# Fused chunked attention and low-rank mixer: blocked q, k, e and u in HBM, transposed on VectorE

## The chip, the cores and the metric

One core of one Trainium2 chip runs the whole program, in one launch. The metric is the device time in microseconds. A core has five engines with queues of their own, each worked through in order: TensorE (PE, with its weight loads shown as PEld), VectorE (DVE), ScalarE (ACT), GpSimd (POOL) and SyncE (SP). SyncE issues nearly all DMAs. All data are float32; `fp32r` is float32 read by TensorE in its faster form, so values are split into a rounded part and a rest ("high" and "low").

## The reference

Eight batches, eight heads, 576 positions of 64 channels. Attention runs within chunks of 64 positions; its output, laid side by side by head, is the input x (576 x 512 per batch) of a mixer:

```python
scores = scale * np.matmul(q_c, k_c.transpose(0, 1, 2, 4, 3))   # per chunk of 64
scores = scores - np.max(scores, axis=-1, keepdims=True)
attn = np.exp(scores)
attn = attn / (np.sum(attn, axis=-1, keepdims=True) + 1e-09)
out = np.matmul(attn, v_c)
...
xt = x.transpose(0, 2, 1)
h = xt @ U @ V                      # along the 576 positions, rank 32
u = x + h.transpose(0, 2, 1)
ch = np.maximum(u @ w_ch1, 0.0) @ w_ch2     # 512 -> 2048 -> 512
return (u + ch).astype(np.float32)
```

U, V, w_ch1 and w_ch2 arrive as 64-bit floats; the kernel makes float32 of their words itself.

## The kernel before

**Tiles.** Batches go in four pairs. A pair has 2 x 576 = 1152 rows, nine tiles (t = 0 to 8) of 128 rows. Three tiles make a group g. The hidden layer is cut into 16 blocks f of 128. The unit of the large work is a block (pair, group, f): `hidden` (L682) does 12 matmuls `h` (three products of high and low parts for four channel blocks), `relu_high` (L696, ScalarE) and `relu_low` (L701, VectorE) make `hh` and `hl`, and `project_out` (L708) adds nine matmuls `o` of the block before. There are 4 x 3 x 16 = 192 blocks.

**Side work per tile.** Attention of a tile (`attention_ops`, L441): load q, k and v; turn q and k so that channels lie on partitions; scores `sc` (16 small matmuls, PE); maximum and subtraction (DVE, two of each); `exp` (ACT); turn e = exp(...) so that keys lie on partitions; `av` (PE); the sums and the scaling into x (DVE). Then `project_ops` (L580) forms y = U-product over five tiles of a batch, from x split into `xh` and `xl`, and `mix_ops` (L634) forms u = x + V-product (`low_rank`, `add`), turns u so that channels lie on partitions (`transposed`), and splits it into `uth` and `utl`, the operands of `h`. So u of a group must be ready, turned and split, before that group's first block.

**How things are turned.** The nine tiles of pair 0 are `early`: q, k, e and u are turned on TensorE with the identity (four 128 x 128 blocks each) into a PSUM bank, and copied out by ScalarE. For the 27 later tiles q and k are first copied inside HBM (`halve`, L379) into arrays by half head (32 channels), from which 8 DMAs per tile and operand put 32 x 32 squares where VectorE's 32 x 32 transposition (`squares`, L458) makes the turned form of them. Such a copy reads and writes pieces of 128 bytes. The e and u of later tiles are turned on TensorE like the early ones (L452 with output `ps_eT`, L656 with output `ut`).

**Order.** The first part (pair 0's attention and mixing, the conversion of 16 weight blocks W0 to W15, and the blocks of groups 0 and 1 of pair 0 between them, `STRETCHES`) is laid out by a small planner (`order`, L146) from written costs and places, and kept as planned. Each weight block is loaded raw by SyncE (`wraw`, two DMAs of 512 KB), then converted by seven VectorE and two ScalarE passes. Pair 1's halving copies are put on SyncE's queue after each block from the fourth on (`HALVES_FROM`), and wait there for the block (`add_manual_dep`). Tiles 0 and 1 of pair 1 are attended at blocks 28 and 30 (`GATES`). From pair 0's group 2 on, a loop (L909) emits one block after the other and in four slots per block a share of a list of side steps made by `attend`, `mixes` and `proj`; the framework's scheduler then decides the final order on each engine from these priorities and its own estimate of when inputs are there.

**Buffers.** Eight slots of one pool (`NS`) hold all turned and raw operands of the side work, ten hold x (`NX`), eight PSUM banks hold all results of TensorE.

Of the kernel before, what the change touches and what calls it, by code (L numbers as in the profile page):

```python
# [21 lines left out]
def kernel(  # L22
# [99 lines left out]
    ROOM = {"bank": 8, "w": NF, "slot": NS, "x": NX, "y": 2, "ut": 2, "h": 2, "mx": 2, "sm": 2}  # L122
# [198 lines left out]
    def w_ops(f, after=None):  # L321
# [15 lines left out]
        for z in range(n):  # L337
            cols = slice(z * size, (z + 1) * size)

            def room(z=z):  # L340
                return wslot((size,), U32, f"wroom_{f}") if n == 1 else slot(U32, f"wroom_{f}_{z}")
# [13 lines left out]
            tag = "w" if n == 1 else "slot"  # L355
# [14 lines left out]

    loaded = {}
# [6 lines left out]
    hidden_last = [None]  # L378

    def halve(b, z, g):  # L380
        d = halves[b, z, g] = dram.tile([S, H * SQ], F32, name=f"half{'qk'[z]}_{b}_{g}")
        moved = nc.sync.dma_start(
            d.rearrange("s (h i) -> s h i", h=H),
            (q, k)[z][b, :, :, g * SQ : (g + 1) * SQ].rearrange("h s i -> s h i"),
        )
        sync = mybir.DependencyInfo(mybir.DependencyClass.Sync, mybir.DependencyReason.DATA)
        tc.add_manual_dep(moved.ins, hidden_last[0].ins.name, sync, reason="after this block")

    def halvings(pr):
        return [lambda b=b, z=z, g=g: halve(b, z, g) for b in (2 * pr, 2 * pr + 1) for z in range(2) for g in range(2)]  # L390

    def load_qk(pr, t):
        n = f"{pr}_{t}"
        if early(pr, t):
            words = wslot((4 * DM,), F32, "qkv_" + n)
            qn, kn = (words[:, z * DM : (z + 1) * DM].rearrange("p (h d) -> p h d", h=H) for z in range(2))
            vn = words[:, 2 * DM : 2 * DM + H * D1].rearrange("p (c a k) -> p c a k", c=2, k=D1)
        else:
            qn = slot(F32, "qn_" + n, (P, P // SQ, P))
            kn = slot(F32, "kn_" + n, (P, P // SQ, P))  # L400
            vn = slot(F32, "vn_" + n, (P, 2, HP, D1))
        nc.gpsimd.memset(vn[:, :, :, D:], 1.0)  # L402
        if not early(pr, t):
            for z, dst in enumerate((qn, kn)):
                for r, m, b, s0 in segments(pr, t):
                    for e in range(2):
                        for g in range(2):
                            x0 = (2 * e + g) * SQ
                            nc.sync.dma_start(
                                dst[x0 : x0 + SQ, r // SQ : (r + m) // SQ, :],  # L410
                                halves[b, z, g][s0 : s0 + m, e * P : (e + 1) * P].rearrange(
                                    "(a j) c -> j a c", j=SQ
                                ),
                            )
            loaded[pr, t] = qn, kn, vn
            return
# [5 lines left out]
    def heads(pr, t, e):  # L422
        return slice(e, None, 2) if early(pr, t) else slice(e * HP, (e + 1) * HP)
# [19 lines left out]

    def attention_ops(pr, t, *after):
        n = f"{pr}_{t}"
        st = {}
        mine = early(pr, t)

# [9 lines left out]
        def squares(z, name):  # L458
            dst = slot(F32, name + n, (P, HP, P))
            nc.vector.transpose(  # L460
                dst.rearrange("p h (a j) -> p h a j", j=SQ),
                loaded[pr, t][z].rearrange("p a (h i) -> p h a i", i=SQ),
# [3 lines left out]
        def evacuate(name):  # L466
            if name[0] == "e":
                dst = slot(F32, name + n, (P, HP, P))
# [22 lines left out]
        def maximum(e):  # L491
            if e == 0:
                st["ex"] = slot(F32, "ex_" + n, (P, HP, 2, C))
# [4 lines left out]
        def subtract(e):  # L498
            mx = st["mx"][:, e, :]
            nc.vector.tensor_sub(st["ex"][:, :, e, :], st["sc"][e], mx.unsqueeze(2).broadcast_to([P, HP, C]))  # L500

        def exp():
            exf = st["ex"].rearrange("p a b k -> p (a b k)")
            nc.scalar.activation(exf, exf, AF.Exp, scale=SCALE)  # L504

# [22 lines left out]
        def scaled(e):  # L528
# [12 lines left out]
        flat = lambda: st["ex"].rearrange("p a b k -> p (a b k)")  # L541
        lq = Op(
            "SP", 3.4 if mine else 5.0, lambda: load_qk(pr, t), *after, take="w" if mine else "slot slot slot", lat=1.6
        )
        if mine:
            tq = Op("PE", 0.55, lambda: transpose(src(0), "qT_"), lq, begun.get((pr, t - 2)), take="bank")
        else:
            tq = Op("DVE", 0.6, lambda: squares(0, "qT_"), lq, begun.get((pr, t - 2)), take="slot")
# [9 lines left out]
        if mine:  # L558
            cq = Op("ACT", 0.58, lambda: evacuate("qT_"), tq, take="w", free="bank")
            tk = Op("PE", 0.55, lambda: transpose(src(1), "kT_"), lq, tq, take="bank")  # L560
            ck = Op("ACT", 0.58, lambda: evacuate("kT_"), tk, cq, free="bank")
            turned = [[tq, cq], [tk, ck]]
        else:
            ck = Op("DVE", 0.6, lambda: squares(1, "kT_"), tq, take="slot")
            turned = [[tq], [ck]]
        sc = Op("PE", 0.62, scores, ck, take="bank bank", free="w" if mine else "slot slot slot slot")
        m0 = Op("DVE", 0.41, lambda: maximum(0), sc, take="slot mx")
# [4 lines left out]
        te = Op("PE", 0.55, lambda: transpose(flat(), "eT_"), ex, take="bank", free="slot")  # L572
        ce = Op("ACT", 0.58, lambda: evacuate("eT_"), te, take="slot", free="bank")
        av = Op("PE", 0.65, values, ce, lv, take="bank bank x", free="slot w" if mine else "slot slot")
# [4 lines left out]
        return [[lq, lv], *turned, [sc, m0, s0, m1, s1, ex], [te, ce], [av, sm, x0, x1]]  # L579
# [4 lines left out]
    def project_ops(pr, e, xs):  # L584
        steps = []
        prev = None
        for i in range(5):
# [3 lines left out]
            def high(i=i, n=n, st=st):  # L591
                st["h"] = slot(F32R, "xh_" + n)
                nc.scalar.copy(st["h"], x_of[pr, i + 4 * e])  # L593

            def low(i=i, n=n, st=st):
                st["l"] = slot(F32R, "xl_" + n)
# [22 lines left out]
            h = Op("ACT", 0.62, high, xs[i + 4 * e], take="slot")  # L619
            lo = Op("DVE", 0.69, low, h, take="slot")  # L620
            prev = Op("PE", 0.47, product, lo, prev, u_done, take="" if i else "bank", free="slot slot")
# [12 lines left out]
    def mix_ops(pr, t, x, ys, after=None, first=None):  # L634
# [22 lines left out]

        def high():
# [23 lines left out]
    def hidden(pr, g, f):  # L682
# [5 lines left out]
        for cc in range(NCC):  # L688
            for z, u in prods:
                hidden_last[0] = nc.tensor.matmul(  # L690
                    ps[:, :GN], lhsT=w[:, z, cc], rhs=u[:, cc, :], start=(n == 0), stop=(n == 3 * NCC - 1)
                )
                n += 1
        return ps
# [78 lines left out]
    HALVES_FROM = 4  # L773
# [36 lines left out]
    second = halvings(1)  # L810
    gates = dict(zip(GATES, range(len(GATES))))
    for g, f0, f1 in STRETCHES:
        for f in range(f0, f1):
# [5 lines left out]
            if blocks >= HALVES_FROM and second:  # L819
                rank[0] = 0  # L820
                in_halves = Op("SP", 0.6, second.pop(0), prev[0], lat=6.0)
            if blocks in gates:
                assert not second
                rank[0] = 0
                attention_ops(1, gates[blocks], prev[0], in_halves)
# [11 lines left out]
    Op("SP", 3.8, lambda: load(1, len(GATES)), prev[0], take="slot slot slot")  # L837
# [13 lines left out]
    to_halve = {}  # L851
# [10 lines left out]
    def step(*group):  # L862
        return lambda: [o.run() for o in group]

    def attend(ts):
        steps = []
        prev = None
        for key in ts:
            i = tiles.index(key)
            _, q, k, sc, et, av = attention_ops(*key)  # L870

            def ahead(i=i):
# [84 lines left out]
```

## Time and profile before

| what | value |
|---|---|
| runs of the kernel | 986.68 us median of 3 (986.33 to 990.02) |
| the profiled execution: its time | 984.5 us |
| its span, first to last instruction | 982.7 us |
| mean granted TensorE clock | 0.990 |
| busy: PE, DVE, ACT | 98%, 45%, 23% of the span |
| first matmul of a hidden block | 64.5 us |
| DMA packets, bytes | 208123, 70.58 MB |

A profile gives each instruction's line in the kernel, its engine, what it writes and reads, and its time. "Idle before, releaser" is how long its engine had stood before it and what ended that. The chain of waits goes back from the last instruction to whatever released each step, so its shares tell what the time was spent on. The clock column is the share of full speed that TensorE was granted. Ends of matmuls are modelled, since they overlap: the chain gives better prices for them than their mean duration does.

### The profile page before, as it was taken

The page shows a single profiled execution, that of the slowest core. Times are in us where ns is not written, and L with a number is a line of the kernel's source. Part 1 is how long each engine was busy: PE and PEld are TensorE (multiplying, and loading weights), DVE is VectorE, ACT ScalarE, POOL GpSimd, SP SyncE. Part 2 cuts the span into 40 slices and gives each one's busy share as a digit, 9 for nine tenths or more (in the row PEclk, how much of TensorE's full clock was granted, in tenths as well). Part 3 has the DMA queues.
Part 4 walks back from the last instruction along what each step waited for, and adds up shares of the span by engine and source line. Part 5 has one row for each costly group of instructions (what it writes and reads, how often), then busy time and mean ns, then how long its engine had stood idle before and what let it go on. Part 6 is the DMA issues. An engine that isn't in the chain of part 4 may idle for free.

```text
span 982.7 us, 16528 instructions
## 1 busy us (share of the span) xinstructions
PE 961.3 (98%) x6854; PEld 835.0 (85%) x6857; DVE 439.5 (45%) x867; ACT 227.5 (23%) x406; POOL 33.7 (3%) x89
## 2 busy tenths in 40 slices
PE   7899899999999999999999999999999999999998
PEld 4569799988888889888888888888888889999997
DVE  5789789874442534233443343333433333211211
ACT  4543333321321211111211221111212121111110
POOL 6500000000000000000000000000000000000000
PEclk8999999999999999999999999999999999999999
DMA  9945964146753121433332111111121000000000
GB/s 218 224 140 97 210 187 139 36 133 112 129 107 89 31 41 52 81 61 86 68 79 62 28 33 37 42 37 48 42 57 33 33 1 1 33 1 1 33 1 33
DMA packets 208123, 70.58 MB, mean 72 GB/s; under 512 B 164768, under 2 KB 200640, under 8 KB 208048
## 3 DMA queue, kind: packets, MB, share of 16 engines
q1 hardware_dynamic: 206528, 66.35, 29.9%
q0 software_dynamic: 1520, 3.17, 1.6%
q8 instruction: 54, 0.88, 0.4%
q14 instruction: 21, 0.17, 0.1%
HBM read 59.98 MB, written 23.67 MB: 85 GB/s over the span
## 4 chain that ended last, share of the span: by engine, by line
PE 91%; DMA 3%; DVE 3%; ACT 1%; SPq 1%; issue 1%; POOL 0%; DVEq 0%; ACTq 0%; POOLq 0%
PE h L690 41%; PE o L716 40%; PE sc L482 2%; PE av L513 2%; PE ut L656 2%; PE ps_eT L452 1%; DMA wraw<-in_moe_w_ch_dram 1%; PE u L644 1%; DMA qkv<-in_k_dram 1%; PE y L604 1%; PE y L605 1%; DMA uraw<-in_moe_U_dram 1%; DMA qkv<-in_v_dram 1%; PE y L611 1%; ACT qkT L474 0%
## 5 line engine op out<-in xcount | busy, mean ns | idle before, releaser
L690 PE MATMUL h<-uth,w 128*128 128x384 f32 x1536 | 424.8, 341 | 0.0
L716 PE MATMUL o<-w,hh 128*128 128x512 f32 x1152 | 359.2, 401 | 3.7 <-ACT hh L698 3.5
L690 PEld LDWEIGHTS h<-uth,w 128*128 128x128 f32 x1536 | 282.1, 188 | 8.2 <-issue 0.2
L703 DVE SCALAR_TENSOR_TENSOR hl<-h,hh 128x384 fp32r<-128x384 f32 x192 | 106.5, 555 | 361.3 <-ACT hh L698 361.1
L690 PE MATMUL h<-utl,w 128*128 128x384 f32 x768 | 260.0, 339 | 0.0
L716 PEld LDWEIGHTS o<-w,hh 128*128 128x128 f32 x1152 | 211.6, 189 | 42.2 <-ACT hh L698 5.6
L716 PE MATMUL o<-w,hl 128*128 128x512 f32 x576 | 217.7, 397 | 0.0
L698 ACT ACTIVATE hh<-h 128x384 fp32r<-128x384 f32 x192 | 94.2, 491 | 499.9 <-PE h L690 499.6
L690 PEld LDWEIGHTS h<-utl,w 128*128 128x128 f32 x768 | 144.8, 189 | 6.1 <-DVE utl L669 0.3
L716 PEld LDWEIGHTS o<-w,hl 128*128 128x128 f32 x576 | 108.7, 189 | 25.8 <-DVE hl L703 0.3
L504 ACT ACTIVATE ex<-ex 128x512 f32<-128x512 f32 x36 | 22.8, 633 | 97.0 <-DVE ex L500 94.0
L496 DVE TENSOR_REDUCE mx<-sc 128x4 f32<-128x256 f32 x72 | 27.9, 417 | 27.5 <-PE sc L482 27.4
L650 DVE TENSOR_TENSOR x<-u,x 128x512 f32<-128x512 f32 x36 | 24.3, 684 | 27.6 <-PE u L644 27.4
L460 DVE STREAM_TRANSPOSE qT<-qn 128x512 f32<-128x512 f32 x27 | 19.1, 708 | 31.8 <-PE y L604 15.6
L669 DVE TENSOR_TENSOR utl<-ut,uth 128x512 fp32r<-128x512 f32 x36 | 24.4, 687 | 19.8 <-ACT uth L664 19.8
L474 ACT COPY eT<-ps_eT 128x512 f32<-128x512 f32 x36 | 21.0, 587 | 42.6 <-PE ps_eT L452 19.8
L597 DVE TENSOR_TENSOR xl<-x,xh 128x512 fp32r<-128x512 f32 x30 | 20.5, 687 | 21.6 <-ACT xh L593 18.4
L500 DVE TENSOR_TENSOR ex<-sc,mx 128x256 f32<-128x256 f32 x72 | 28.0, 416 | 1.2 <-DVE mx L496 0.5
L664 ACT CAST uth<-ut 128x512 fp32r<-128x512 f32 x36 | 20.9, 587 | 32.2 <-PE ut L656 32.1
L532 DVE TENSOR_TENSOR x<-av,sm 128x256 f32<-128x256 f32 x72 | 27.1, 417 | 1.1
L402 POOL MEMSET vn<- 128x8 f32 x27 | 3.0, 112 | 685.1 <-PE y L605 205.3
L728 DVE TENSOR_TENSOR x<-o,x 128x512 f32<-128x512 f32 x36 | 23.1, 684 | 4.9 <-PE o L716 4.8
(84 smaller groups left out, 552.3 us busy)
## 6 DMA issues: line engine op xcount, KB each, us to landing
wraw<-in_moe_w_ch_dram SPq DMA_DIRECT2D x32, 512.0 KB, 7.1
out_dram<-x SPq DMA_DIRECT2D x36, 256.0 KB, 2.2
halfq<-in_q_dram SPq DMA_DIRECT2D x12, 576.0 KB, 6.3
halfk<-in_k_dram SPq DMA_DIRECT2D x12, 576.0 KB, 6.1
vn<-in_v_dram SPq DMA_DIRECT2D x108, 64.0 KB, 2.4
qn<-halfq SPq DMA_DIRECT2D x96, 64.0 KB, 2.0
kn<-halfk SPq DMA_DIRECT2D x96, 64.0 KB, 2.0
qkv<-in_v_dram POOLq DMA_DIRECT2D x36, 64.0 KB, 6.3
```

Of the source, the lines that this page charges most:

```text
L474: nc.scalar.copy(dst.rearrange("p a b -> p (a b)"), st[name])
L496: nc.vector.reduce_max(mx, st["sc"][e], axis=AX.X)
L500: nc.vector.tensor_sub(st["ex"][:, :, e, :], st["sc"][e], mx.unsqueeze(2).broadcast_to([P, HP, C]))
L504: nc.scalar.activation(exf, exf, AF.Exp, scale=SCALE)
L532: nc.vector.tensor_mul(by_head[:, heads(pr, t, e), :], st["av"][e][:, :, 0:D], st["sm"][:, e].unsqueeze(2).broadcast_to([P, HP, D]),)
L650: nc.vector.tensor_add(x, st["u"], x)
L669: nc.vector.tensor_sub(ul[:, :, js], st["t"].rearrange("p (c t) -> p c t", c=NCC), uh[:, :, js])
L690: hidden_last[0] = nc.tensor.matmul(ps[:, :GN], lhsT=w[:, z, cc], rhs=u[:, cc, :], start=(n == 0), stop=(n == 3 * NCC - 1))
L698: nc.scalar.activation(hh, ps[:, :GN], AF.Relu)
L703: nc.vector.scalar_tensor_tensor(hl, ps[:, :GN], 0.0, hh, op0=ALU.max, op1=ALU.subtract)
L716: nc.tensor.matmul(acc[g, j], lhsT=h[:, js], rhs=w2[f][:, z], start=(first and i == 0), stop=(final and i == 2),)
L728: nc.vector.tensor_add(x, ps, x)
```

## The change

Later tiles' q, k, e and u are all turned by VectorE's 32 x 32 transposition, out of blocks in HBM that 128 partitions read in long pieces.

- `plain(pr, t)` names the tiles that stay with TensorE for q, k and e: the nine of pair 0, and tiles 0 and 1 of pair 1. These two load q and k directly from the inputs now (`load_qk`) and turn them on TensorE. All u of pairs 1 to 3, 27 tiles, go the new way, and e of 25 tiles.
- The halving copies write one array per pair and operand, ordered by chunk of 64 rows, half head and row, in copies of half the former size (one for each half of the heads too), 8 per batch. A tile's q is then one DMA in which each partition reads two pieces of 1 KB, and so is its k.
- e: the subtraction writes by half heads, `spread_e` puts the tile into HBM in 512-byte pieces (L459 of the new file) and `fetch`es it back with 2 KB per partition (L400), and `square_e` turns it on VectorE (L539).
- u: `put_u` writes the tile in four DMAs of 128-byte pieces (L454), `fetch_u` brings it back, `square_u` turns it into `uT` (L709), from which the same two splitting passes read, from SBUF now and not from PSUM.
- The eight common slots become pools by use (`SLOTS`: three for q and k, two for v, one each for e, eT, us and uT), x has nine places. `xh` and `xl` of the projection use uT's and us's single buffer.
- Halvings begin after block 13 in place of 4, two of the smaller ones after every other block, and each waits for the block before the one it is emitted behind. Those of pairs 2 and 3 are single steps of the side list.
- The side steps stand in lists of words (`LATER`, `FIRST`): `t` turns q and k, `s` is scores to exp and the put of e (with the load of the next tile behind the scores, and the `av` of the tile before last in front), `q` the turn of e, `a` the last `av`, `p` a projection step, `l` the V-product, addition and put of u, `f` its fetch, `u` its turn and split, `h` a halving, `.` nothing. The words of a group are spread over its 64 slots less 8 (`TAIL`).

```diff
+    SLOTS = {"qk": 3, "e": 1, "eT": 1, "vn": 2, "us": 1, "uT": 1}
...
+    def plain(pr, t):
+        return pr == 0 or (pr == 1 and t < len(GATES))
...
+        moved = nc.sync.dma_start(
+            halves[pr, z][odd * n : (odd + 1) * n, 2 * e + g].rearrange("n s (h i) -> n s h i", i=SQ),
+            (q, k)[z][b, e * HP : (e + 1) * HP, :, g * SQ : (g + 1) * SQ].rearrange("h (n s) i -> n s h i", s=C),
+        )
...
+        tc.add_manual_dep(moved.ins, hidden_last[-2].ins.name, sync, reason="after this block")
...
+    def fetch(kept, dst):
+        nc.sync.dma_start(dst, kept.rearrange("z (j a) c -> (z j) a c", a=P // SQ))
+        return dst
...
+                nc.sync.dma_start(
+                    dst.rearrange("p (n a) c -> p n a c", n=2),
+                    halves[pr, z][2 * t : 2 * t + 2].rearrange("n x (j a) c -> (x j) n a c", a=2),
+                )
...
+    def put(src, name, by_channel=False):
+        kept = dram.tile([P // SQ, P, P], F32, name=name + "d")
+        if by_channel:
+            for c in range(NCC):
+                nc.sync.dma_start(
+                    kept.rearrange("z p (c i) -> p z c i", i=SQ)[:, :, c],
+                    src.rearrange("p (c z i) -> p z c i", c=NCC, i=SQ)[:, :, c],
+                )
+        else:
+            nc.sync.dma_start(kept.rearrange("z p c -> p z c"), src.rearrange("p (z c) -> p z c", c=P))
+        return kept
...
+        if own:
+            te = Op("PE", 0.55, lambda: transpose(flat(), "eT_"), ex, take="bank", free=tag_e)
+            ce = Op("ACT", 0.58, lambda: evacuate("eT_"), te, take=tag_eT, free="bank")
+        else:
+            te = Op("SP", 2.5, spread_e, ex, lat=3.0)
+            ce = Op("DVE", 0.71, square_e, te, take="eT", free="e")
...
+        if pr > 0:
+            pu = Op("SP", 2.0, put_u, ad, lat=2.0)
+            fe = Op("SP", 2.0, fetch_u, pu, take="us", lat=2.0)
+            tr = Op("DVE", 0.71, square_u, fe, take="uT", free="us")
+            hi = Op("ACT", 0.59, high, tr, take="" if j else "ut")
+            lo = Op("DVE", 0.69, low, hi, free="uT")
+            return [[lr, ad, pu], [fe], [tr, hi, lo]]
...
-    HALVES_FROM = 4
+    TAIL = 8
+    HALVES_FROM = 13
...
+            if blocks >= HALVES_FROM and blocks % 2 == 1 and second:
+                rank[0] = 0
+                for _ in range(2):
+                    Op("SP", 0.6, second.pop(0), prev[0], lat=3.0)
...
+    LATER = {
+        0: "t6 q5 s6 l3 h f3 h t7 q6 s7 u3 p0 p1 h t8 h q7 s8 p2 p3 h . . q8 a8 p4 . l4 . f4 l5 . . u4 f5 . . . u5",
...
```

More of the change, by code (lines that the diff above doesn't have):

```diff
@@ L693, in hidden @@
                 n += 1
+        hidden_last.append(o)
         return ps
@@ L809 @@
     blocks = 0
-    second = halvings(1)
+    second = halvings(2) + halvings(3)
     gates = dict(zip(GATES, range(len(GATES))))
@@ L848 @@
     manual.__exit__(None, None, None)
-    to_halve = {}
+    assert not second
+    to_halve = [w for b in range(4, B) for w in halvings(b)]
     tiles = [(pr, t) for pr in range(NPAIR) for t in range(NT)]
@@ L860, in flush @@
                 finish(pr, g, f, j, ps)
[L862 to L872, printed above, removed]
-                if i + 1 < len(tiles) and tiles[i + 1] not in loaded:
-                    load(*tiles[i + 1])
-                pr, t = tiles[i]
-                if pr + 1 < NPAIR:
-                    todo = to_halve.setdefault(pr + 1, halvings(pr + 1))
-                    for _ in range(-(-len(todo) // max(1, NT - 1 - t))):
-                        todo.pop(0)()
-            steps += [ahead, step(*q)] + ([prev[0]] if prev else [])
-            steps += [step(*k)] + ([prev[1]] if prev else []) + [step(*sc)]
-            prev = step(*et), step(*av)
-        return steps + (list(prev) if prev else [])
@@ L886, in mixes, with begin_next @@
-    def mixes(pr, ts):
-        steps = []
-        st = [[step(*z) for z in mix_ops(pr, t, None, [None, None])] for t in ts]
-        for i in range(len(st) + 1):
-            steps += ([st[i][0]] if i < len(st) else []) + ([st[i - 1][1]] if i else [])
-        return steps
-    def proj(pr, e):
-        return [step(*z) for z in project_ops(pr, e, [None] * NT)[0]]
+    behind = []
+    def begin_next(i):
+        if i + 1 < len(tiles) and tiles[i + 1] not in loaded:
+            load(*tiles[i + 1])
@@ new lines, in attend @@
+    def attend(pr, t, what):
+        if what == "turn":
+            _, q, k, soft, square, av = attention_ops(pr, t)
+            behind.append((soft, square, av))
+            return [*q, *k]
+        if what == "square":
+            return behind[0][1]
+        if what == "last":
+            return behind.pop(0)[2]
+        soft = behind[-1][0]
+        done = behind.pop(0)[2] if len(behind) > 1 else []
+        i = tiles.index((pr, t))
+        return [*done, soft[0], lambda: begin_next(i), *soft[1:]]
@@ new lines, with go @@
+    mixing = {}
+    def go(pr, g, word):
+        if word == ".":
+            return
+        if word == "h":
+            if to_halve:
+                to_halve.pop(0)()
+            return
+        kind, i = word[0], int(word[1:])
+        if kind in "tsqa":
+            at = pr + 1 if g else pr
+            if at < NPAIR:
+                do(attend(at, i, {"t": "turn", "s": "scores", "q": "square", "a": "last"}[kind]))
+            return
+        at = pr + 1 if g == 2 else pr
+        if at == NPAIR:
+            return
+        if kind == "p":
+            e = int(g == 0)
+            if i == 0:
+                mixing["p"] = project_ops(at, e, [None] * NT)[0]
+            do(mixing["p"][i])
+        elif kind == "l":
+            mixing[i] = mix_ops(at, i, None, [None, None])
+            do(mixing[i][0])
+        else:
+            do(mixing[i]["lfu".index(kind)])
@@ L917 @@
                 slots += 1
-                while done < len(steps) and done * (NF * 4 - 6) < len(steps) * slots:
-                    steps[done]()
+                while done < len(steps) and done * (NF * 4 - TAIL) < len(steps) * slots:
+                    go(pr, g, steps[done])
                     done += 1
```

161 lines of the change are left out of this document (86 added, 75 removed), and 2 rows, old and new, of the table LATER.

## The prediction

> **What bounds the kernel now.** I read the page first, then the busy time by stretches, then the chain of waits, then the queue of SyncE, and last the groups of instructions. The page says who is full:
>
> ```profile
> span 982.7 us, 16528 instructions
> ...
> PE 961.3 (98%) x6854; PEld 835.0 (85%) x6857; DVE 439.5 (45%) x867; ACT 227.5 (23%) x406; POOL 33.7 (3%) x89
> ...
> PE 91%; DMA 3%; DVE 3%; ACT 1%; SPq 1%; issue 1%; POOL 0%; DVEq 0%; ACTq 0%; POOLq 0%
> ```
>
> TensorE is busy for 98% of the span, and 91% of the chain that ended last is its work. So what leaves TensorE shortens the program, unless a new wait takes its place. The average hides one stage, though. By stretches (length, then busy time of PE, PEld, DVE, ACT and POOL, then the granted clock, the share of the DMA engines, GB/s):
>
> ```profile
> 70.00:98.00 28.00, 27.39 (x141) 24.45 (x140) 27.09 (x34) 10.52 (x15) 0.00 (x0) 1.00 0.44 83
> 98.00:125.00 27.00, 23.46 (x104) 19.76 (x103) 21.35 (x27) 8.61 (x11) 0.00 (x0) 0.90 1.22 207
> 122.00:125.00 3.00, 3.00 (x9) 2.33 (x9) 2.96 (x5) 1.05 (x1) 0.00 (x0) 0.50 1.34 175
> 300.00:375.00 75.00, 75.00 (x548) 65.30 (x547) 29.48 (x64) 16.14 (x31) 0.34 (x3) 1.00 0.27 59
> ```
>
> From 300 to 375 us TensorE never rests, while VectorE works 29.5 of 75 us and the DMA engines are a quarter full. From 70 to 98 us, where weights are still being converted, VectorE is nearly full as well (27.1 of 28). And from 98 to 125 us TensorE did 104 matmuls where 28 us before held 141, the DMA engines were overfull (1.22), and the clock fell to half. The chain of waits (start, length, what) shows why:
>
> ```profile
> 72.57 4.18 PE o L716 x18
> 76.75 4.22 PE h L690 x24
> ...
> 103.45 5.36 DMA wraw<-in_moe_w_ch_dram
> ...
> 114.05 4.98 DMA wraw<-in_moe_w_ch_dram
> ...
> 120.66 4.21 PE o L716 x9
> 124.87 5.04 PE h L690 x24
> ...
> 202.43 0.44 PE ps_eT L452 x4
> 202.87 0.44 PE ut L656 x4
> ```
>
> The chain leaves TensorE here and runs over two loads of raw weights. The queue of SyncE and the longest wait of TensorE say what held them:
>
> ```profile
> 104.00 6.24 SPq L382 DMA_DIRECT2D halfq<-in_q_dram  x2
> ...
> 148.20 0.37 SPq L326 DMA_DIRECT2D wraw<-in_moe_w_ch_dram  x1
> ```
>
> ```profile
> PE o L716 <- ACT hh L698: 3.5, 1, 3.5
> ```
>
> Two halving copies (q and k split by half heads into HBM) blocked the queue for 6.2 us, where a weight load takes 0.37 us to issue when nothing is in its way. TensorE then stood still for 3.5 us once. Nothing like it comes later.
>
> **The change, part by part.** *Transposes off TensorE.* For the 25 later tiles the transposition of e goes, for the 27 tiles of pairs 1 to 3 that of u: 52 groups of four. Tiles 0 and 1 of pair 1 now turn q and k on TensorE: 4 groups come. The chain prices a group of either kind at 0.44 us of TensorE's path. Net 48 x 0.44 = 21.1 us, all of it on the engine that sets the end. On TensorE's queue, a tile of e (tile 3 of pair 2) before, late in pair 1's second group:
>
> ```order
> L690 MATMUL h_1_1_13_4481<-uth_1_1_3630,w_13_1806 128x384 x2
> L452 MATMUL ps_eT_2_3_4501<-ident_69,ex_2_3_4471 128x128 x4
> L716 MATMUL o_1_3_3953<-w_13_1806,hh_1_1_13_4494 128x512 x2
> L716 MATMUL o_1_4_3957<-w_13_1806,hh_1_1_13_4494 128x512 x2
> L716 MATMUL o_1_5_3961<-w_13_1806,hh_1_1_13_4494 128x512 x2
> ```
>
> And a tile of e now, in the first group of pair 2, ahead of the product with v:
>
> ```order
> L779 MATMUL o_2_0_5281<-w_7_1394,hh_2_0_7_5613 128x512 x2
> L779 MATMUL o_2_1_5286<-w_7_1394,hh_2_0_7_5613 128x512 x2
> L779 MATMUL o_2_2_5290<-w_7_1394,hh_2_0_7_5613 128x512 x2
> L779 MATMUL o_2_0_5281<-w_7_1394,hl_2_0_7_5615 128x512
> L779 MATMUL o_2_1_5286<-w_7_1394,hl_2_0_7_5615 128x512
> L779 MATMUL o_2_2_5290<-w_7_1394,hl_2_0_7_5615 128x512
> L779 MATMUL o_2_0_5281<-w_8_1456,hh_2_0_8_5640 128x512
> L550 MATMUL av0_2_8_5652<-vn_2_8_5391,eT_2_8_5647 64x65 x2
> ```
>
> No transposition stands there any more; what remains is whether eT is there when `av` comes.
>
> *What VectorE and ScalarE get.* The groups of instructions (busy, mean ns):
>
> ```profile
> L500 DVE TENSOR_TENSOR ex<-sc,mx 128x256 f32<-128x256 f32 x72 | 28.0, 416 | 1.2 <-DVE mx L496 0.5
> L496 DVE TENSOR_REDUCE mx<-sc 128x4 f32<-128x256 f32 x72 | 27.9, 417 | 27.5 <-PE sc L482 27.4
> L532 DVE TENSOR_TENSOR x<-av,sm 128x256 f32<-128x256 f32 x72 | 27.1, 417 | 1.1
> L669 DVE TENSOR_TENSOR utl<-ut,uth 128x512 fp32r<-128x512 f32 x36 | 24.4, 687 | 19.8 <-ACT uth L664 19.8
> L650 DVE TENSOR_TENSOR x<-u,x 128x512 f32<-128x512 f32 x36 | 24.3, 684 | 27.6 <-PE u L644 27.4
> ...
> L504 ACT ACTIVATE ex<-ex 128x512 f32<-128x512 f32 x36 | 22.8, 633 | 97.0 <-DVE ex L500 94.0
> ...
> L460 DVE STREAM_TRANSPOSE qT<-qn 128x512 f32<-128x512 f32 x27 | 19.1, 708 | 31.8 <-PE y L604 15.6
> ```
>
> 48 more transpositions of 0.708 us are 34 us for VectorE, where by the row at 300 us it is busy for two fifths of the time. ScalarE loses 21 copies. Both lie beside TensorE's work and cost nothing in themselves. New access patterns of the same size may be slower, between nothing and twice 0.7 us a piece; I take nothing, as q and k are turned in strided views already.
>
> *The weight stage.* The halvings now begin at block 13 in place of 4, and two of half the size come after every other block. On SyncE's queue before:
>
> ```order
> L382 DMA halfq_2_0_1120<-in_q_dram 4608x1x32
> L382 DMA halfq_2_1_1162<-in_q_dram 4608x1x32
> L326 DMA wraw_6_1166<-in_moe_w_ch1_dram 128x4x256
> L330 DMA wraw_6_1166<-in_moe_w_ch2_dram 128x1024
> L382 DMA halfk_2_0_1190<-in_k_dram 4608x1x32
> L382 DMA halfk_2_1_1232<-in_k_dram 4608x1x32
> L326 DMA wraw_7_1236<-in_moe_w_ch1_dram 128x4x256
> ```
>
> and now:
>
> ```order
> L327 DMA wraw_9_1357<-in_moe_w_ch1_dram 128x4x256
> L331 DMA wraw_9_1357<-in_moe_w_ch2_dram 128x1024
> L389 DMA halfq_1_1400<-in_q_dram 9x256x32 x2
> L327 DMA wraw_10_1414<-in_moe_w_ch1_dram 128x4x256
> L331 DMA wraw_10_1414<-in_moe_w_ch2_dram 128x1024
> L327 DMA wraw_11_1477<-in_moe_w_ch1_dram 128x4x256
> ```
>
> Weights 6 to 9 are no longer behind halvings, and each weight has half the former traffic ahead of it. The stall is worth: 3.5 us of standing; then nine `o` in 4.21 us against half of 4.18 for eighteen, 2.1 lost; then 24 `h` in 5.04 against 4.22, 0.8 lost: 6.4 us. I take all of it; the bounds are 0 and 6.4.
>
> *New waits.* A tile's e goes to HBM and back, u too. These DMAs are priced by (KB, median us from issue to landing):
>
> ```profile
> out_dram<-x SPq DMA_DIRECT2D x36, 256.0 KB, 2.2
> halfq<-in_q_dram SPq DMA_DIRECT2D x12, 576.0 KB, 6.3
> halfk<-in_k_dram SPq DMA_DIRECT2D x12, 576.0 KB, 6.1
> vn<-in_v_dram SPq DMA_DIRECT2D x108, 64.0 KB, 2.4
> qn<-halfq SPq DMA_DIRECT2D x96, 64.0 KB, 2.0
> ```
>
> For e: two maxima and two subtractions (1.7), exp (0.6), out (2.2), back (2.2), turn (0.7): 7.4 us. The shortest distance that TensorE's order leaves is that of tile 8: 24 `h` and 20 `o` between its last `sc` and first `av`, 4.2 + 4.6 = 8.8 us. Other later tiles have 10 to 46 us. For u the tight place is tile 3, whose turned form must leave its single buffer before the first `y` product of the second half: 24 `h`, 27 `o` and two groups of small matmuls (one `sc`, one `av`) stand between, 4.2 + 6.3 = 10.5 us without the latter. Its chain: addition (0.7), four puts and a fetch of e ahead of the fetch (five issues of 0.37, 1.9), landing of the last (2.4), back (2.2), turn, split and next split (four passes of 0.6 to 0.7, 2.7): 9.9 us, and a halving of 288 KB in the same queue, which by the rows at 576 and 64 KB adds up to (6.3 - 2.0) / 2 = 2.1. So at six places (tiles 8 and 3 in three pairs) the data come about when TensorE does: between 0 and 2 us each, I take 1, together 6 us. What queues behind the wait is seen on VectorE's order, first group of pair 2:
>
> ```order
> L766 SCALAR_TENSOR_TENSOR hl_2_0_2_5311<-h_2_0_2_5296,hh_2_0_2_5309 128x384
> L539 STREAM_TRANSPOSE eT_2_6_5327<-es_2_6_5249 128x4x128
> L709 STREAM_TRANSPOSE uT_2_3_5416<-us_2_3_5294 128x4x128
> L766 SCALAR_TENSOR_TENSOR hl_2_0_3_5344<-h_2_0_3_5329,hh_2_0_3_5342 128x384
> ```
>
> A late fetch holds `hl` of the next block, which `o` needs; `hl` has the time of one `h` block, some 2 us, to spare.
>
> A put of u goes out in pieces of 128 bytes. The Trainium skill, page "DMA: Bandwidth & Descriptors", section "Specifications", wants 512 bytes for full rate; by its rule the puts would be nearer the halving row (6.3 us for 4608 pieces of 128 bytes) than the row of v. By that row the four puts (2048 pieces) would end some 1 to 2 us later, which is the upper end of what I allow at tile 3.
>
> *The rest.* q and k of a tile come in 2 DMAs in place of 8 or more, one pool of 8 slots becomes several of 1 to 3, x has 9 places for 10. Loads still start a tile ahead; I put this at 0, with 3 us either way for the start and 3 for the two tiles that cross into the new layout: no row shows them, and 3.5 us is the longest wait that TensorE has anywhere now.
>
> **The sum.** -21.1 - 6.4 + 6 = -21.5 us. The profiled execution took 984.5 us, 1.8 over its span; the median of the runs is 986.68, 2.2 above that. I take the difference off the median: 965 us.
>
> **The rivals.** *The round trips come late and TensorE cools (slower).* If fetches are late by 3.5 us, each such wait costs what the one above did, 6.4 us, since the clock row at 122 us reads 0.50 after it. The saving of 27.5 is gone after 27.5 / 6.4 = 4.3 such waits. With nine (tiles 3, 5 and 8 in three pairs) the time is 986.7 - 27.5 + 57.6 = 1017 us. For it: single buffers and one queue for all DMAs. Against: no DMA of up to 256 KB has a median over 2.4 us here, and most tiles have over 10 us. The Trainium skill, page "TensorE: Matmul & The Clock Gate", section "Part 1: The HAM clock gate", halves the clock after an idle window of about 3.4 us; the trace agrees (3.5 us, then 0.50). By that rule shorter waits cost only their length.
>
> *The weight stage keeps its stall.* VectorE is at 27.1 of 28 us there, and halvings still pass between weights 10 to 15. Then 965 + 6.4 = 972 us.
>
> *The waits don't come at all.* Then 965 - 6 = 959 us.
>
> *Nothing is gained.* If `o` waits for VectorE's longer queue wherever a transposition went, the time stays at 986.7. Against: 29.5 busy of 75 us.
>
> **How the numbers follow.** My forecast 0.56; no new waits 0.16; the stall kept 0.13; no gain 0.06; slower 0.09. Half a per cent (4.9 us) is about what a measurement of this kernel can tell from no change. The first three are faster by more than that: 0.85; the same 0.06; slower 0.09. The range leaves out the last two. Low: 959 less the 6 us of the rest, 953. High: 972 with 2 us in place of 1 at six places, 978, and 3 of the rest, 981; beyond that lie the cases left out.
>
> **What would show it.** No `ps_eT` or `ut` groups beyond 11 and 9, 102 transpositions on VectorE near 0.7 us, TensorE's busy time down by about 20; the clock at 1.00 from 98 to 125 us and weights issued in 0.4 us; waits of `av` and `y` for VectorE under 2 us. Several waits over 3 us with a clock below 1 from 200 us on, or fetches landing after 5 us, would prove me wrong.

## The result, and the profile after

The changed kernel takes 1000.4 us (median of 4 runs, 995.3 to 1003.2), the kernel before 987.0 in runs beside it. The ratio is 1.0124, with a 95% interval of 1.0078 to 1.0169: slower by 1.2%, where 965 us and faster was forecast. The profiled execution took 1000.45 us.

The page of the changed kernel, its span, its engines and the chain that ended last:

```profile
span 998.6 us, 16154 instructions
...
PE 944.5 (95%) x6660; PEld 821.2 (82%) x6663; DVE 486.7 (49%) x915; ACT 213.2 (21%) x385; POOL 33.8 (3%) x89
...
PE 72%; DMA 13%; SPq 5%; DVE 5%; issue 2%; ACT 2%; POOL 1%; DVEq 0%; POOLq 0%; ACTq 0%
```

TensorE is busy for 16.8 us less than before (961.3), as it should be, but the span is 16 us longer. The chain says where to look: TensorE's share fell from 91% to 72%, and DMA, SyncE's queue and VectorE hold 23% in its place.

Two rows of stretches cover the same work, from the end of pair 0's second group to the last additions (length, busy PE, PEld, DVE, ACT, POOL, clock, DMA share, GB/s). The kernel before:

```profile
216.00:979.00 763.00, 761.21 (x5258) 670.04 (x5258) 260.95 (x561) 144.22 (x273) 2.58 (x23) 1.00 0.22 48
```

The changed kernel, that stretch and two groups out of it:

```profile
219.00:995.00 776.00, 745.29 (x5082) 656.58 (x5082) 309.01 (x610) 128.18 (x247) 2.70 (x24) 0.99 0.36 83
308.00:390.00 82.00, 75.55 (x505) 66.53 (x505) 34.60 (x67) 14.72 (x28) 0.34 (x3) 0.96 0.42 91
544.00:626.00 82.00, 74.33 (x502) 65.46 (x501) 33.96 (x67) 14.51 (x28) 0.34 (x3) 0.96 0.41 90
```

Before, TensorE stood still for 763.0 - 761.2 = 1.8 us of this main part; now for 776.0 - 745.3 = 30.7. In the first group of pairs 1 and 2 it stands for 6.5 and 7.7 of 82 us, and the granted clock is 0.96 there. The waits of TensorE from 216 to 996 us name what it stood for (us in all, times, longest):

```profile
PE y L647 <- ACT xh L636: 9.8, 3, 3.9
PE av L550 <- DVE eT L539: 8.8, 5, 3.4
PE av L550 <- issue: 4.6, 3, 2.3
PE o L779 <- DVE hl L766: 3.2, 3, 1.2
PE o L779 <- ACT hh L761: 2.3, 4, 1.6
```

The kernel before has 0.6 us of waits in that part. `av` waits at tiles 2, 6 and 8 of the pairs, `y` at the first product of the second half, whose copy `xh` waits for the place of tile 3's uT. The early groups end later in this execution as well: the last addition of pair 0's second group begins at 218.4 us, before at 215.3.

The chain of the changed kernel at tile 2 of pair 3 (start, length, what) shows one such wait being built:

```profile
666.92 0.70 PE av L550 x32
...
667.71 0.12 POOL vn L414
667.83 2.30 SPq L438
...
670.90 3.95 DMA kn<-halfk
...
674.95 0.72 DVE kT L480
...
675.69 0.36 SPq L417
...
676.17 3.04 DMA es_2d<-ex
...
679.24 2.62 DMA es<-es_2d
...
681.88 1.09 DVE eT L539
```

And ScalarE's timeline there:

```profile
672.07 0.63 ACT L531 ACTIVATE ex<-ex 128x512 f32<-128x512 f32 x1 [3.92 <-DVE ex L523]
```

e was ready at 672.7 us. Its put went out at 676.2, because SyncE's queue first held two loads of v that waited for `av`, then the load of k behind them, then (after two more of v) a load of q that waited for a buffer which the turn of k sets free. Then 3.04 us out, 2.62 back and 1.09 for the turn: 10.3 us from e to eT, 3.5 of them in the queue. TensorE's order leaves 12.8 us between the end of `sc` and the start of `av` of this tile (its wait of 2.1 us taken off); the data, with maxima and exp, took 14.7.

The groups of VectorE's turns (busy, mean ns, idle time before):

```profile
L539 DVE STREAM_TRANSPOSE eT<-es 128x512 f32<-128x512 f32 x25 | 27.4, 1096 | 84.1 <-DMA es<-es_3d 14.6
L709 DVE STREAM_TRANSPOSE uT<-us 128x512 f32<-128x512 f32 x27 | 29.6, 1097 | 60.9 <-DMA us<-us_2d 12.6
L480 DVE STREAM_TRANSPOSE kT<-kn 128x512 f32<-128x512 f32 x25 | 17.8, 712 | 41.2 <-DMA kn<-halfk 41.2
```

The new turns take 1.10 us where the old ones take 0.71, and VectorE stands for 186 us in front of these three, all of it for DMAs, with the next blocks' `hl` queued behind it.

### The profile page after: what moved, and what is told of

It is laid out like the page before. It is cut to its first block, busy times and chain, and to the rows that moved or that the text cites. A ratio compares the mean times of both kernels' runs of the same rounds, so it can differ in the third digit from the quotient of the medians.

```text
span 998.6 us, 16154 instructions
## 1 busy us (share of the span) xinstructions
PE 944.5 (95%) x6660; PEld 821.2 (82%) x6663; DVE 486.7 (49%) x915; ACT 213.2 (21%) x385; POOL 33.8 (3%) x89
## 4 chain that ended last, share of the span: by engine, by line
PE 72%; DMA 13%; SPq 5%; DVE 5%; issue 2%; ACT 2%; POOL 1%; DVEq 0%; POOLq 0%; ACTq 0%
PE o L779 32%; PE h L752 32%; SPq L438 3%; DMA kn<-halfk 2%; PE av L550 2%; PE sc L502 1%; DVE eT L539 1%; SPq L454 1%; DMA es_2d<-ex 1%; PE u L687 1%; DMA us_3d<-x 1%; DMA es<-es_2d 1%; DMA us<-us_3d 1%; SPq L417 1%; DMA vall<-vrows 1%
## 5 line engine op out<-in xcount | busy, mean ns | idle before, releaser
L752 PE MATMUL h<-uth,w 128*128 128x384 f32 x1536 | 413.2, 339 | 0.0
L779 PEld LDWEIGHTS o<-w,hh 128*128 128x128 f32 x1152 | 214.4, 190 | 43.2 <-ACT hh L761 5.3
L539 DVE STREAM_TRANSPOSE eT<-es 128x512 f32<-128x512 f32 x25 | 27.4, 1096 | 84.1 <-DMA es<-es_3d 14.6
L709 DVE STREAM_TRANSPOSE uT<-us 128x512 f32<-128x512 f32 x27 | 29.6, 1097 | 60.9 <-DMA us<-us_2d 12.6
L719 ACT CAST uth<-uT 128x512 fp32r<-128x512 f32 x27 | 16.8, 620 | 124.5 <-DVE uT L709 124.5
L480 DVE STREAM_TRANSPOSE kT<-kn 128x512 f32<-128x512 f32 x25 | 17.8, 712 | 41.2 <-DMA kn<-halfk 41.2
L550 PEld LDWEIGHTS av<-vn,eT 64*64 64x64 f32 x864 | 17.3, 133 | 25.0 <-issue 25.0
L550 PE MATMUL av<-vn,eT 64*64 64x65 f32 x864 | 21.9, 224 | 13.5 <-DVE eT L539 8.8
L636 ACT CAST xh<-x 128x512 fp32r<-128x512 f32 x30 | 18.6, 619 | 61.4 <-DVE x L569 55.5
(95 smaller groups left out, 562.3 us busy)
```

The source lines that it names most:

```text
L539: nc.vector.transpose(st["eT_"].rearrange("p h (j a) -> p a h j", j=SQ), st["es"].rearrange("p a (h i) -> p a h i", i=SQ))
L550: nc.tensor.matmul(ps[e][cs, hp * D1 : (hp + 1) * D1], lhsT=st["eT_"][rows, hp, cs], rhs=vn[rows, c, hp, :], start=True, stop=True,)
L709: nc.vector.transpose(uT.rearrange("p (c j a) -> p a c j", c=NCC, j=SQ), st["us"].rearrange("p a (c i) -> p a c i", i=SQ))
L752: o = nc.tensor.matmul(ps[:, :GN], lhsT=w[:, z, cc], rhs=u[:, cc, :], start=(n == 0), stop=(n == 3 * NCC - 1))
L779: nc.tensor.matmul(acc[g, j], lhsT=h[:, js], rhs=w2[f][:, z], start=(first and i == 0), stop=(final and i == 2),)
```

## The experiments

Theories. **A**: the round trips of e and u come late. It has two forms: **A1**, their DMAs wait in SyncE's queue; **A2**, they are too long in themselves for the distance that the order leaves. **B**: loads of v block SyncE's queue, for k and all else. **C**: the slow strided turn. **S**: the late start of the first blocks (70.8 us against 64.5) is a loss of its own. Each time stands beside runs of the kernel before on the same chip, and a ratio is to those.

**One round trip or both taken back (three runs).** e turned on TensorE again, and laid out as in the early tiles for that:

```diff
-        if own:
+        if True:
             te = Op("PE", 0.55, lambda: transpose(flat(), "eT_"), ex, take="bank", free=tag_e)
```

> The changed kernel, with e turned on TensorE again as before (25 groups of four, +11.0 us of TensorE); u still goes through HBM. Theory A, the round trips of e and u come late: the standing time in front of av (13.8 us), half of that in front of o (3 of 6, where hl queues behind eT on VectorE) and their share of the slow clock (5) go, 1000.4 - 22 + 11 = 989 us, and the clock from 308 to 390 us, now 0.96, is 1.00. Theory B, the waits come from SyncE's blocked queue (kn behind vn) and only show up under av: they stay, 1000.4 + 11 = 1011 us.

Measured: 993.0 us, ratio 1.0051 (1.0022 to 1.0080). The waits of `av` are gone but for 0.8 us; those of `y` stay, 3.6 us each, with a clock of 0.98 from 308 to 390, not 1.00. A gives the size within 4 us, B does not:

```profile
PE y L647 <- ACT xh L636: 7.1, 2, 3.6
PE y L647 <- DVE hl L766: 3.7, 1, 3.7
```

u turned on TensorE again:

```diff
-        if pr > 0:
+        if False:
             pu = Op("SP", 2.0, put_u, ad, lat=2.0)
```

> The changed kernel, with u turned on TensorE again as before (27 groups of four, +11.9 us of TensorE); e still goes through HBM. Theory A, the round trips come late: the standing time in front of y (10.4 us), 2 of o and 3 of slow clock go, 1000.4 - 15.4 + 11.9 = 997 us, and the waits of av stay at 10 us or more. Theory B, SyncE's blocked queue: all stays, 1012 us; or, if the five DMAs of u a tile were what held e's fetches back, av's waits go too, 983 us.

Measured: 986.6 us, ratio 1.0000 (0.9980 to 1.0019). The waits of `y` are gone and those of `av` stay, somewhat smaller (10.1 us in place of 13.4). This is 10 us better than the waits of `y` alone would give, and short of the 983 us at which the waits of `av` would go too. u's five DMAs a tile held e's back in part, but that is 3.3 us; the rest was not taken apart.

```profile
PE av L550 <- DVE eT L539: 8.0, 7, 3.2
PE av L550 <- issue: 2.1, 3, 0.8
```

Both edits together:

> The changed kernel, with e and u both turned on TensorE again (+22.9 us of TensorE), the new loads, lists and pools kept. Theory A, the round trips are the whole loss: all standing over 0.5 us in the main part (31.4 us) and the slow clock behind it (7.8) go, 1000.4 - 39 + 23 = 984 us, which is the time before less the 6.4 us of the weight stage and plus the 6.3 us of the late start. Theory B, the new list of side work and SyncE's queue make the waits: over 1000 us.

Measured: 987.6 us, ratio 0.9999 (0.9987 to 1.0011). In the main part TensorE stands for 763.0 - 755.7 = 7.3 us, at a clock of 1.00:

```profile
217.00:980.00 763.00, 755.66 (x5290) 670.02 (x5290) 257.88 (x559) 142.88 (x273) 2.71 (x24) 1.00 0.22 49
```

So the round trips are the loss against the kernel before, and B as the whole cause falls. This kernel still has the late halvings, which alone bring some 6 us (below), and is no faster than the kernel before; so the new loads of q and k, the pools, the list and the start cost about as much together (an estimate).

**The turn.** The two new turns write their columns side by side. The rows of a tile then stand in another order than the reference's, so this run prices the turn and gives no usable result:

```diff
-                st["eT_"].rearrange("p h (j a) -> p a h j", j=SQ), st["es"].rearrange("p a (h i) -> p a h i", i=SQ)
+                st["eT_"].rearrange("p h (a j) -> p a h j", j=SQ), st["es"].rearrange("p a (h i) -> p a h i", i=SQ)
...
-                uT.rearrange("p (c j a) -> p a c j", c=NCC, j=SQ), st["us"].rearrange("p a (c i) -> p a c i", i=SQ)
+                uT.rearrange("p (c a j) -> p a c j", c=NCC, j=SQ), st["us"].rearrange("p a (c i) -> p a c i", i=SQ)
```

> The changed kernel, but the turns of e and u write their 32 columns side by side (the order of the rows in a tile is then not the reference's), same DMAs. Theory C, the strided turn (1.10 us in place of 0.71) is the cost: 52 x 0.39 = 20 us of VectorE go, the turns take 0.71 us, and the time falls by 15 us or more, below 986 us. Theory A, the way through HBM is late: each trip is 0.4 us of some 8 shorter, 16 gaps x 0.4 = 6 us, about 994 us. If the turn's price is covered: 1000 us.

Measured: 994.9 us, ratio 1.0073 (1.0047 to 1.0100). The turns fell to 0.71 us:

```profile
L709 DVE STREAM_TRANSPOSE uT<-us 128x512 f32<-128x512 f32 x27 | 19.2, 710 | 57.4 <-DMA us<-us_7d 10.4 <-DMA us<-us_2d 8.1 <-DMA us<-us_8d 7.8
L539 DVE STREAM_TRANSPOSE eT<-es 128x512 f32<-128x512 f32 x25 | 17.8, 712 | 84.5 <-DMA es<-es_3d 15.1 <-DMA es<-es_2d 14.4 <-DMA es<-es_6d 13.6
```

20 us of VectorE's work went and some 5 us of time. That is about 0.4 us, by which the turn became shorter, for each of a dozen waits (an estimate), as it would be if the turn counts as part of a trip and not as work. C falls as the main cause.

**Which queue (two runs).** The round trips issued by GpSimd (the put of u by channels in the same way):

```diff
-            nc.sync.dma_start(kept.rearrange("z p c -> p z c"), src.rearrange("p (z c) -> p z c", c=P))
+            nc.gpsimd.dma_start(kept.rearrange("z p c -> p z c"), src.rearrange("p (z c) -> p z c", c=P))
...
-        nc.sync.dma_start(dst, kept.rearrange("z (j a) c -> (z j) a c", a=P // SQ))
+        nc.gpsimd.dma_start(dst, kept.rearrange("z (j a) c -> (z j) a c", a=P // SQ))
```

> The changed kernel, with all DMAs that take e and u to HBM and back issued by GpSimd's queue in place of SyncE's; the loads of q, k, v and the halvings stay on SyncE. Theory A1, the round trips are late because their DMAs stand in SyncE's queue behind others that wait (es_2d of pair 3: e ready at 672.7 us, put issued at 676.2; es_6d of pair 2: put issued at 547.0, fetch at 553.0): at least half of the standing in front of av, y and o (30 us) and half of the slow clock (8) go: 1000.4 - 19 = 981 us or less. Theory A2, the trips are late by their own length (landing 3 us, fetch 2.6, turn 1.1) against the distance left in the list: less than 8 us go, 992 us or more.

Measured: 987.2 us, ratio 0.9995 (0.9978 to 1.0013), 13 us better than the changed kernel, where A1 asked for 19 or more and A2 for less than 8: between the two forms, and neither is the whole. The Trainium skill, page "DMA: Bandwidth & Descriptors", section "Issuing engines are not separate DMA queues", says that issuing from several engines saves only the sequencer's time for issuing, usually a small one. Here the issues of the trips themselves take 0.33 to 0.55 us on SyncE and 0.54 to 0.77 on GpSimd, so nothing was saved on them; what was saved is the time in which a DMA ready to go stands behind one that waits. `av` waits 6.9 us in place of 13.4, at tile 2 no longer; `y` still waits, now up to 5.7 us at once:

```profile
PE y L647 <- ACT xh L636: 11.2, 3, 5.7
PE av L550 <- DVE eT L539: 6.1, 6, 1.6
```

Only the later tiles' loads of v issued by GpSimd:

```diff
-                queue = nc.gpsimd if early(pr, t) else nc.sync
+                queue = nc.gpsimd if early(pr, t) or not plain(pr, t) else nc.sync
```

> The changed kernel, with only the loads of v of the tiles in the new layout issued by GpSimd's queue. Theory B, kn and the puts of e stand behind the loads of v on SyncE: the waits of VectorE for kn (41 us before) fall below 15, the standing in front of o and sc (7 us) and of av at tiles 2 and 8 (about 10 us) goes, 1000.4 - 15 = 985 us. Theory A2, the trips' own length: 998 us or more.

Measured: 988.9 us, ratio 1.0021 (1.0004 to 1.0037). That is 10 us less by the ratios. VectorE's waits for k fell from 41 to 22 us, not to 15; `av` waits 8.4 us in place of 13.4, `y` 8.9 in place of 9.8. So the loads of v are a large part of what holds the trips back.

```profile
DVE kT L480 <- DMA kn<-halfk: 22.2, 11, 4.4
```

**The trip's own length.** TensorE turns only u of tile 3 and e of tile 8:

```diff
-        if pr > 0:
+        if pr > 0 and t != 3:
             pu = Op("SP", 2.0, put_u, ad, lat=2.0)
...
+        here = own or t == 8
-        if own:
+        if here:
             te = Op("PE", 0.55, lambda: transpose(flat(), "eT_"), ex, take="bank", free=tag_e)
...
-        0: "... q7 s8 p2 p3 h . . q8 a8 p4 ..."
+        0: "... q7 s8 p2 p3 q8 h . . a8 p4 ..."
```

> The changed kernel, with TensorE turning only u of tile 3 and e of tile 8 of each pair (6 groups of four, +2.6 us of TensorE), the two places that the prediction named; all other round trips stay on SyncE. Theory A2, at these places the trip's own length is more than the distance: the waits of y (10.4 us) and of av at tile 8 (3), and about half of the slow clock (4) go: 1000.4 - 17.4 + 2.6 = 986 us; the waits of av at tiles 2 and 6 stay (2 to 3.5 us each in five places). Theory A1, only the queue counts: the two places were late because of it, the others too, and the waits move on: 995 us or more.

Measured: 983.7 us, ratio 0.9960 (0.9946 to 0.9974): six of the 52 groups taken back bring 16 us. `y` and `av` of tile 8 no longer wait; `av` still waits for tiles 2 and 6:

```profile
PE av L551 <- DVE eT L540: 6.5, 4, 3.3
```

The edit also takes these trips' DMAs out of SyncE's queue, so alone it does not part length from queue; the runs with both causes treated do (below).

**The early groups (two runs).** The conversion of moe_V early:

```diff
+        if z == "V":
+            for o in ops[begin:]:
+                if o.eng == "DVE":
+                    o.rank = 0.5, o.rank[1]
...
-        o = Op("POOL", 2.0, spread, o, take="w", lat=2.5)
+        o = Op("POOL", 2.0, spread, o, take="w", lat=7.0)
```

> The changed kernel, with the conversion of moe_V placed early on VectorE by its rank, and the planner told 7 us for the landing of its spread. Theory S, the late start is a loss of its own: the first h block begins at 64 to 66 us in place of 70.8, and the time falls by 5 to 6 us, 994.5 us. Rival, the weights' conversion sets the pace of the stage anyhow: the start moves and the end of the stage (205.5 us) does not, 1000 us.

Measured: 998.7 us, ratio 1.0109 (1.0075 to 1.0143), not to be told from the changed kernel. The first block begins at 63.3 us, 7.5 earlier, and pair 0's second group ends only 2 us earlier (216.5 against 218.4). The kernel before with late halvings:

```diff
-    HALVES_FROM = 4
+    HALVES_FROM = 13
```

> The kernel before, with one number changed: the halving copies begin at block 13 in place of 4, one after each block. The term of the prediction for the weight stage, alone: 987 - 6.4 = 980.6 us, no standing of TensorE of 3.5 us and a clock of 1.00 from 98 to 125 us. Rival, VectorE, full in that stage, holds the blocks: 985 to 987 us.

Measured: 982.2 us, ratio 0.9937 (0.9913 to 0.9961): 6.2 us by the ratio (3.9 to 8.6). The profiled execution is the slowest of the five, 983.9 us. Its stretches, against 55.77 and 75.00 us of busy TensorE in the kernel before:

```profile
65.00:125.00 60.00, 59.31 (x299) 52.47 (x298) 56.80 (x72) 23.36 (x33) 0.00 (x0) 1.00 0.20 71
125.00:200.00 75.00, 72.84 (x382) 64.58 (x381) 64.47 (x96) 23.60 (x37) 0.11 (x1) 0.98 0.75 151
```

The stall goes (+3.5), and in this execution a smaller one comes where the halvings now lie (-2.2).

**Both causes treated.** The edits of GpSimd's queue, of the two tiles and of moe_V together:

> The changed kernel with both causes treated: the round trips of e and u on GpSimd's queue, u of tile 3 and e of tile 8 of each pair turned on TensorE, moe_V converted early. If queue and trip length are separate causes that add up: from the 987 us with the trips on GpSimd's queue, y's waits (11.8), av's at tile 8 (5) and the slow clock (4) go, 2.6 come, 2 for the start go: 967 us, faster than the kernel before by 2%. If something else waits next: 975 to 985 us.

Measured: 968.8 us, ratio 0.9820 (0.9799 to 0.9841), faster than both kernels. The main part, and the waits of TensorE in it:

```profile
219.00:963.00 744.00, 735.09 (x5072) 652.76 (x5070) 304.73 (x600) 131.08 (x250) 116.09 (x187) 1.00 0.35 82
```

```profile
PE av L551 <- DVE eT L540: 2.3, 2, 1.8
PE h L753 <- DVE x L570: 2.1, 4, 0.6
PE h L753 <- DVE hl L767: 1.9, 2, 1.0
```

TensorE stands for 8.9 us in place of 30.7, at a mean clock of 1.00. The two gains add up: 12.9 parts in a thousand for the queue, 16.4 for the two tiles, 30.4 for both and moe_V. So the tight places cost as much when the trips have GpSimd's queue: their length is a cause beside SyncE's queue. At tile 2 of pair 3, GpSimd's timeline has the put right behind exp, and the fetch right behind the put's landing:

```profile
652.29 0.76 POOL L459 DMA_DIRECT2D es_2d<-ex  x1 [6.70 <-ACT ex L532]
656.09 0.54 POOL L400 DMA_DIRECT2D es<-es_2d  x1 [3.04 <-DMA es_2d<-ex]
```

The same without the edit of moe_V:

> The mixed kernel without the early conversion of moe_V (start as in the changed kernel). Theory S, the late start of 6 us is a loss of its own: 968.8 + 5 = 974 us. Rival, the weights set the pace of the stage, whenever it starts: 969 to 971 us, and the last tile of group 0 of pair 0 ends as early as in the mixed kernel, at about 205 us.

Measured: 969.0 us, ratio 0.9822 (0.9800 to 0.9844); the second group of pair 0 ends at 216.9 us, in the mixed kernel at 218.5. S falls: what the start gains is lost again before the weights are done. These ends scatter: in the nine executions whose early part is the changed kernel's, this group ends between 215.2 and 219.1 us, so that neither this 1.6 nor the 3.1 against the kernel before means much. The mixed kernel with the loads of v on GpSimd in place of the round trips:

> The other way to empty SyncE's queue: the loads of v on GpSimd, the round trips on SyncE, and again u of tile 3 and e of tile 8 on TensorE and moe_V early. If it is only the loads of v that hold the round trips back, this is as good as the mixed kernel: 967 to 971 us. If the other DMAs of SyncE (halvings, q and k) hold them too, the waits of av at tiles 2 stay (2.5, 1.2 and 1.8 us with v alone moved): 973 to 977 us.

Measured: 973.1 us, ratio 0.9863 (0.9842 to 0.9884). `av` waits for tile 2 of each pair (2.3, 2.0 and 1.2 us) and nowhere else:

```profile
PE av L551 <- DVE eT L540: 5.6, 3, 2.3
```

So v is not the only thing ahead of the trips in SyncE's queue. The changed kernel shows what else: at tile 2 of pair 1, whose wait is its longest of `av`, exp ended at 225.8 us and the put went out at 230.0, behind two halvings and a load of k that held the queue for 3.3 and 2.9 us.

## Why the prediction was wrong, step by step

**The step that failed is "new waits".** It allowed 6 us: six places, 1 us each. The main part stands for 28.9 us more than before. Three things in that step were wrong.

*The places.* It named tiles 8 and 3 of each pair and passed over the others with "10 to 46 us". Tile 2 with its 12.8 us is one of those, tile 6 another. By the single waits, TensorE stood for 12.5 us at the named places (9.8 at `y`, 2.7 at tile 8) in place of 6, for 10.0 at tiles 2 and 6 in place of nothing, and for 6.5 in front of `o` and `sc`. The distance was right; the need was not.

*The length of a trip.* Medians of the profile before were taken for out and back, 2.2 us each, and 0.7 for the turn: 5.1. The chain above shows 3.04, 2.62 and 1.09: 6.8. The allowance for the turn ("between nothing and twice 0.7 us a piece; I take nothing") held the measured 0.4 us, at the wrong value; the views of q and k that were the reason wrote their columns side by side in the kernel before, and the new ones write every fourth. The two tiles taken back on TensorE show what the length costs at the tight places: 16 us.

*The queue.* The prediction counted u's own puts at tile 3, but for e it let the put leave when exp ends. It did not ask what stands ahead on SyncE, which holds loads that wait for TensorE or for a buffer that VectorE frees: 3.5 us at tile 2 of pair 3. The round trips on another queue show what that costs: 13 us. The issues ahead of a DMA, counted for u, had to be counted for e too, with what they wait for.

Tile 3 has both, length and queue. The chain of the changed kernel, pair 2:

```profile
549.67 2.15 SPq L454
...
553.54 2.93 DMA us_3d<-x
...
556.54 2.58 DMA us<-us_3d
...
559.14 1.10 DVE uT L709
```

The prediction had 1.9 us for all issues; the addition ended at 548.7 and the last put went out at 553.5, 4.8 us later. `y` began at 562.3, after 2.3 us of waiting for tile 6 and 3.9 of its own.

**TensorE cools: the rival was right in kind.** It was given 9%: round trips late, the clock down, slower. It asked for nine waits of 3.5 us and gave 1017 us. Measured were three waits of over 3 us (3.4 at `av`, 3.7 and 3.9 at `y`), a dozen of 0.6 to 2.3, and 1000 us. Its argument against, that no DMA of up to 256 KB has a median over 2.4 us, passes over rows of the same view: the loads of q for pair 0, 256 KB, have 9.7, those of v on GpSimd, 64 KB, 6.3. Stretches of the changed kernel behind two of the long waits (3.4 us, ended at 237; 3.7, ended at 325) and three shorter ones (1.4, ended at 590; 2.1, ended at 683; 2.2, ended at 798):

```profile
237.00:241.00 4.00, 4.00 (x72) 3.59 (x73) 3.29 (x12) 0.62 (x1) 0.11 (x1) 0.63 0.58 86
326.00:331.00 5.00, 5.00 (x16) 4.07 (x15) 4.41 (x13) 1.25 (x2) 0.00 (x0) 0.58 0.31 85
590.00:595.00 5.00, 5.00 (x54) 4.53 (x55) 2.50 (x8) 1.11 (x2) 0.11 (x1) 1.00 0.25 56
683.00:688.00 5.00, 4.76 (x79) 3.97 (x80) 2.95 (x10) 0.00 (x0) 0.11 (x1) 1.00 0.06 14
798.00:800.00 2.00, 1.96 (x4) 1.33 (x5) 1.91 (x7) 0.62 (x1) 0.00 (x0) 0.50 0.42 108
```

After the long waits the clock is 0.6, after two of the shorter ones 1.00; but after the wait of 2.2 us it is 0.50. So the length of one wait doesn't decide, and the prediction's "shorter waits cost only their length" does not hold here. In pair 2 the clock is at half from 559 us on, when `y` had stood for only 0.5 of its 3.9 us:

```profile
558.00:559.00 1.00, 0.40 (x28) 0.27 (x19) 0.00 (x0) 0.00 (x0) 0.11 (x1) 0.95 0.52 192
559.00:560.00 1.00, 0.00 (x0) 0.00 (x0) 0.85 (x1) 0.00 (x0) 0.00 (x0) 0.50 0.67 113
```

There `av` had waited 2.3 us just before, and between the two waits lay only the small products of `av` and `sc`, 1.2 us. By single microseconds, the four falls of the clock in this kernel's main part came 4.0 to 4.5 us after the large products gave way to waits and small products (in the last, three `o` lay among them); at 590 and 683 us large products were back after 2.2 and 2.4 us. The rival had the mechanism and the sign, with too many long waits.

**The transposes off TensorE: right.** With both on TensorE, its busy time of the main part is 755.7 us; in the mixed kernel, with 46 groups fewer, 735.1. That is 20.6 / 46 = 0.45 us a group, against 0.44. In the changed kernel, with six groups fewer still, it is 745.3 and not 732.4. Work at half the clock explains some 7 of these 13 us (14.8 us of it, by single microseconds behind the four falls; an estimate); the rest is open, and ends of matmuls are modelled.

**The weight stage: right by itself, given back in this kernel.** The late halvings alone give the kernel before 6.2 us (3.9 to 8.6), as the term said (6.4). Stretches of the changed kernel:

```profile
0.00:65.00 65.00, 49.07 (x708) 32.58 (x712) 40.86 (x106) 29.55 (x53) 30.94 (x64) 0.87 1.02 220
65.00:125.00 60.00, 58.11 (x321) 50.79 (x321) 57.33 (x79) 23.02 (x32) 0.00 (x0) 1.00 0.24 75
125.00:200.00 75.00, 74.77 (x376) 67.07 (x374) 64.50 (x94) 25.87 (x41) 0.00 (x0) 1.00 0.77 155
```

Against the kernel before (53.37, 55.77 and 75.00 busy), the stage gains 2.3 us and the time ahead of it loses 4.3: the conversion of moe_V was planned some 5 us later on VectorE, and its spread landed 7.41 us after its issue. But moving that conversion did not help, twice. What sets the end of these groups is therefore still open: VectorE is busy for 57.3 of 60 us there, but TensorE for 58.1 of 60 and 74.8 of 75, and neither was tried. With moe_V early, TensorE's longest waits from 62 to 220 us include those for pair 1's direct loads of q and k (1.6 and 0.9) and for converted weights (0.8 and 0.5).

**VectorE's 48 turns "cost nothing": right as work.** 20 us of VectorE's time taken away gave 5 us, about what the shorter trips account for.

**The sum.** Forecast -21.5; measured +16.0 by the profiled executions. Of the 37.5 between them, 22.9 are standing beyond the 6 allowed. The early groups are 7.7: they end 3.1 later in this execution, where 6.4 earlier was forecast, less 1.8 for the four groups that came, which lie there. The rest, about 7, is TensorE's busy time in the main part: 15.9 us less and not 52 x 0.44 = 22.9, which is about what the half clock took (7.4, the estimate above).

## What to carry to other kernels

A step that goes through HBM is priced from the moment its data are ready to the moment its reader may start, with the whole queue of its issuing engine in between; every DMA ahead of it that waits for a buffer or a compute engine is part of its length. Check that length against every consumer's distance in the order, not only the shortest, and leave the few tight ones on the old path: here 6 of 52 groups back on TensorE and another queue for the rest turned +1.2% into -1.8%. And a wait of TensorE can cost more than its length: in the changed kernel the clock was at half behind waits of 2.2 to 3.9 us that stood beside small products, and at full behind waits of 1.4 and 2.1 us after which the large products were soon back.

## What the runs showed of the hardware

- A turn of 128x512 on VectorE took 0.70 to 0.71 us when it wrote its columns side by side or every second one (q and k), and 1.10 us when it wrote every fourth. The Trainium skill, page "SBUF — State Buffer", section "Door 1: The DMA port swizzle (why `[64,N]` ≈ `[32,N]`)", has lines of 16 bytes that want two accesses each: every second f32 gives two, every fourth gives one. The runs agree that two accesses a line are free and one is not; the section has no price, and where it gives 4 fp32 as how far one can stride for free, a stride of 4 was not free here.
- At tile 2 of pair 3, 256 KB from SBUF to HBM took 3.04 us from issue to landing and 2.62 us back. On GpSimd's queue 3.80 us passed from the put's issue, itself 0.76, to the fetch's (652.29 to 656.09).
- The spread of moe_V, four copies of 72 KB issued from 44.2 to 46.9 us, landed 7.41 us after the last of them was issued (46.36 to 53.77).
